# The weight decode by way of a PSUM bank, and another table of ranks, in an attention and two-FFN kernel

## The chip, the cores and the metric

One core of a Trainium2 chip. The metric is the device time of one launch in microseconds; a kernel's time is the median of its runs.

## The reference

Four batches of eight heads, sequence 1152, head width 64. Queries are averaged in pairs, so 576 rows of queries meet 1152 keys. The attention's output, 2304 tokens of width 512, goes through two feed-forward layers.

```python
q_pool = q.reshape(B, H, S // 2, 2, D).mean(axis=3)
scores = scale * np.matmul(q_pool, k.transpose(0, 1, 3, 2))
attn = np.exp(scores - max); attn = attn / (sum + 1e-09)
x = (attn @ v) as (B * S/2, H * D)
g = s * relu(x @ w_in) ** 2 + b;  x = g @ w_out            # d_ff 2048
out = (1 / (1 + exp(-(x @ w_gate))) * (x @ w_val)) @ w_out2  # d_ff 1536
```

## The kernel before

All matmuls run on operands that are split in two, a high part and the rest, and each product is made of three matmuls (high by high, high by low, low by high; `mm3`, lines 537 to 540). The five weight matrices arrive as 64-bit floats, in pairs of 32-bit words, and are decoded on the chip.

**The decode** (`decode`, line 481) handles one tile of 128 x 512 weights. A DMA on SP's queue brings the words into a buffer `raw` (three of them). Then, on the upper words, a clamp on GpSimd or VectorE ("w top", line 496) and a multiplication by a power of two on ScalarE ("w scale", line 499, in place); on the lower words a shift on VectorE ("w low", line 500); then two steps on VectorE that put the bits together: "w join" (line 503) and "w sign" (line 506). Both read the scaled upper words and the lower words and write the lower words. "w hi" (line 462) and "w lo" (line 472) split the result into the tile `w` that TensorE loads. There are 104 decodes: 32 for the first feed-forward layer in batch 0, whose results are also written to DRAM ("w keep") and fetched from there for the other batches ("w fetch", line 520, issued on GpSimd's queue), and 72 for the second layer.

**The order** of all instructions on all engines is written by a planner when the program is built. Each step is added with an engine, a duration, what it reads and writes, and a rank. `Plan.order` (line 229 on) walks through time; a free engine takes, among its ready steps for which buffers are free (`fits`, line 242), the one with the lowest rank. The base ranks are FE 0 (feed-forward), DE 0.5 (decode), AT 1 (attention), SK 2, FP 3. The table `MOVED` (line 42 on) has for each named step a pair that is added to the rank and to the place in the list. A step with the flag `port` on VectorE is held back while GpSimd is busy, and taken then only if no other step is ready (lines 272 to 286); a GpSimd step waits for the end of such a VectorE step (line 281).

**PSUM** has eight banks of 128 x 512 words. The planner hands them out by tag; a tag has a limit of its own (`ROOM`: ps 4, pr 8, pm 1, acc 5, ff 6, p2 3), and all together take at most eight. Tags in `LOOSE` may be taken out of turn.

**The course.** Batch 0's attention runs with rows of queries on the partitions (`pair_rows`, tags pr and acc), batches 1 to 3 with keys on the partitions (`scores`, `half_head_sums`, tags ps, pm, acc). The first layer (`ffn1`, tag ff) of batch b is put between the attention of batch b + 1. When the attention is done, `ffn2` (tag p2) handles batches 0 and 1, then `ffn1` handles batch 3, then `ffn2` batches 2 and 3. From about 840 us on there is no attention.

Of the kernel before, what the change touches and what calls it, by code (L numbers as in the profile page):

```python
# [11 lines left out]
F32 = mybir.dt.float32  # L12
F32R = mybir.dt.float32r
AF = mybir.ActivationFunctionType
ALU = mybir.AluOpType
U32 = mybir.dt.uint32
# [9 lines left out]
    w=4, raw=3, xy=2, xx=1, r=2, g=4,  # L26
    qn=1, kn=1, vn=1, qT=2, kT=2, vt=2, st=6, pp=6,
    sg=2, mx=2, mc=2, r9=1, x=1, s=2, rs=1, rr=1,
    yy=1, yl=1, h=4, fo=9,
    ps=4, pr=8, pm=1, acc=5, ff=6, p2=3, bank=8,  # L30
)

DIRECT = (1, 2)
BANKS = {"pr", "ps", "pm", "acc", "ff", "p2"}
LOOSE = {"pr", "ps", "ff", "p2", "r"}


MOVED = {
    "q load": (-0.5, 114),
    "k load": (46, 79),  # L40
    "v load": (58.5, 89),
    "v hi": (-18, -97),
    "v lo": (60, -156),
    "q add": (0, -97),
    "q twice": (0, -7),
    "pr qT": (0, 53),
    "pr q hi False": (23, -93),
    "pr q lo False": (24.5, 3),
    "pr q hi True": (45.5, 50),
    "pr q lo True": (5, 36),  # L50
    "pr kT": (-5, 44),
    "pr k hi": (2, -112),
    "pr k lo": (-5, 116),
    "s b load": (15, 94),
    "r qk 1": (0, 35),
    "r max": (36, 97),
    "r - max": (-29, -40),
    "r exp": (60, -57),
    "r pT": (-23, 13),
    "r p": (0, 52),  # L60
    "r p hi": (17, -107),
    "r p lo": (-25.5, -51),
    "r pv": (-38, 107),
    "r pT hi": (0, 70),
    "r pT lo": (47, -75),
    "r o": (-40, 39),
    "r x add": (40, -62),
    "r qk 2": (-1.5, -71),
    "r sums": (0.5, 106),
    "r sums eps": (-4, 9),  # L70
    "r 1 / sums": (-8, 75),
    "r spread": (-38, 44),
    "r rows": (0, -92),
    "r rows mid": (0, 108),
    "r x / sums": (-1.5, 74),
    "r x / sums mid": (60, 35),
    "r end": (0, 96),
    "ps qT": (24, 13),
    "ps q hi False": (60, 90),
    "ps q lo False": (6, -123),  # L80
    "ps kT": (10, 16),
    "ps k hi": (36.5, -29),
    "ps k lo": (-1, 88),
    "xx hi": (58, -86),
    "xx lo": (2.5, 93),
    "w load": (-12, 6),
    "w top": (-17, 81),
    "w scale": (-3, 17),
    "w low": (-20.5, -68),
    "w join": (9, 116),  # L90
    "w sign": (-25.5, -42),
    "w hi": (-40, 42),
    "w lo": (-28.5, -87),
    "w keep": (-1, 29),
    "one": (-39, -96),
    "ff xx up": (58, 135),
    "ff relu": (0, 72),
    "square": (-40, 76),
    "g hi": (27.5, -76),
    "g lo": (-10.5, 98),  # L100
    "ff down": (57, 43),
    "ff y": (9, 84),
    "column sum": (0, -65),
    "ff y add": (15.5, 115),
    "bias": (13.5, -34),
    "y bias": (-3, 137),
    "y store": (-33, -12),
    "qk": (44.5, 68),
    "s copy": (34.5, 24),
    "s max": (14, 33),  # L110
    "max T": (0, 53),
    "max": (20.5, 103),
    "max rows": (41.5, -120),
    "s - max": (14.5, 67),
    "exp": (0, -7),
    "p hi": (-40, -44),
    "p lo": (-7.5, -102),
    "pv hi": (-10.5, -118),
    "pv lo": (49.5, -31),
    "sums": (41, -60),  # L120
    "x": (36.5, 0),
    "sums out": (10, -13),
    "sums in": (5, -102),
    "1 / sums spread": (-16.5, 16),
    "1 / sums out": (60, -32),
    "1 / sums in": (2.5, -82),
    "x / sums": (0, 63),
    "1 / sums": (27.5, -20),
    "w fetch": (-35.5, -18),
    "w come": (-20.5, 6),  # L130
    "x store": (44, -24),
    "turn": (20, -21),
    "yy load": (-40, -79),
    "yy hi": (0, 50),
    "yy lo": (0, -39),
    "p2 yy up": (4.5, 6),
    "gate": (8, -90),
    "gate val": (-25.5, -72),
    "h hi": (0.5, 90),
    "h lo": (-40, -43),  # L140
    "down 2": (-21, 31),
    "out": (-5, -6),
    "out add": (0, -59),
    "out store": (-2, 45),
    "xx load": (0, 48),
    "p2 xx up": (0, -49),
    "p2 relu": (0, -7),
    "p2 down": (0, 24),
    "p2 y": (-10, -68),
    "p2 y add": (40, -54),  # L150
}


# [193 lines left out]
def kernel(  # L347
# [14 lines left out]
    nc = tc.nc  # L362
# [25 lines left out]

    plan = Plan(ROOM, LOOSE, BANKS, MOVED)

# [5 lines left out]
    ones, zero, eps = (values[:, i:i + 1] for i in range(3))  # L396
# [7 lines left out]
    bias = const.tile([P, KC], F32, name="bias")  # L404
# [14 lines left out]
    def slot(pool, tag, shape, dtype=F32, view=lambda t: t):  # L419
        uid[0] += 1  # L420
        name = f"{tag}_{uid[0]}"
        return plan.slot(tag, lambda k: view(pools[pool].tile(shape, dtype, tag=f"{tag}{k}", bufs=1, name=name)))
# [9 lines left out]
    def bank(tag):  # L432
        return plan.slot(tag, lambda k: banks[:, k])
# [13 lines left out]
    def act(name, n, issue, r, w, rank, sbuf=True):  # L447
        plan.add(name, "ACT", (95 if sbuf else 50) + 0.833 * n, issue, r, w, rank)

    def dve(name, n, issue, r, w, rank, fast=False, port=None):  # L450
        plan.add(name, "DVE", 70 + (0.52 if fast else 1.04) * n, issue, r, w, rank, port=fast if port is None else port)

    def shared(name, n, issue, r, w, rank, pool, act=None, fast=False, more=0):

        other = {"DVE": 70 + (0.52 if fast else 1.04) * n} if act is None else {"ACT": 95 + act * n}
        alts = {**{e: t + more for e, t in other.items()}, "POOL": 105 + pool * n + more}
        plan.add(name, alts, 0, issue, r, w, rank, port=True)

    def copy_sb(name, n, out, in_, r, w, rank):
        def issue(e):  # L460
            if e == "ACT":
                nc.scalar.copy(out=out(), in_=in_())  # L462
            else:
                nc.gpsimd.tensor_scalar(out=out(), in0=in_(), scalar1=1.0, scalar2=0.0, op0=ALU.mult, op1=ALU.add)

        shared(name, n, issue, r, w, rank, 0.95, act=0.833)
# [4 lines left out]
    def tt_sb(name, n, out, in0, in1, op, r, w, rank):  # L471
        shared(name, n, lambda e: ENGINE[e].tensor_tensor(out=out(), in0=in0(), in1=in1(), op=op), r, w, rank, 2.15)  # L472
# [4 lines left out]
    def dma(name, n_bytes, issue, r, w, rank):  # L477
        plan.add(name, "SP", max(n_bytes / 360.0, 500), issue, r, w, rank)


    def decode(src, w, gate, rank):

        raw = slot("dec", "raw", [P, 512, 2], U32)
        low, top = (raw, 0), (raw, 1)

        def words(i):
            return raw.t[:, :, i]

        def fetch():
            if len(src.shape) == 3:  # L490
                nc.sync.dma_start(out=raw.t.rearrange("p (k f) t -> p k (f t)", f=P), in_=src)
            else:
                nc.sync.dma_start(out=raw.t.rearrange("p f t -> p (f t)"), in_=src)

        dma("w load", P * 4096, fetch, gate, [low, top], rank)
        shared("w top", 512, lambda e: ENGINE[e].tensor_scalar(  # L496
            out=words(1).bitcast(F32), in0=words(1).bitcast(F32), scalar1=F64_TOP, scalar2=-F64_TOP, op0=ALU.min, op1=ALU.max,
        ), [], [top], rank, 1.08, fast=True)
        act("w scale", 512, lambda: nc.scalar.mul(words(1).bitcast(F32), words(1).bitcast(F32), 2.0 ** -112), [], [top], rank)  # L499
        dve("w low", 512, lambda: nc.vector.tensor_scalar(  # L500
            out=words(0), in0=words(0), scalar1=29, scalar2=None, op0=ALU.logical_shift_right,
        ), [], [low], rank, True)
        dve("w join", 512, lambda: nc.vector.scalar_tensor_tensor(
            out=words(0), in0=words(1), scalar=3, in1=words(0), op0=ALU.logical_shift_left, op1=ALU.bitwise_or,
        ), [top], [low], rank, port=True)
        dve("w sign", 512, lambda: nc.vector.scalar_tensor_tensor(
            out=words(0), in0=words(1), scalar=0x80000000, in1=words(0), op0=ALU.bitwise_and, op1=ALU.bitwise_or,
        ), [top], [low], rank, port=True)
        copy_sb("w hi", 512, lambda: w.t[:, 0, :], lambda: words(0).bitcast(F32), [low], [(w, 0)], rank)
        tt_sb("w lo", 512, lambda: w.t[:, 1, :], lambda: words(0).bitcast(F32), lambda: w.t[:, 0, :].bitcast(F32), ALU.subtract,  # L510
              [low, (w, 0)], [(w, 1)], rank)
# [69 lines left out]
    def load_x(b):  # L581
        return load_split("fx", "xx", x_d[b], [("x_d", b, i) for i in range(2 * NP)])
# [503 lines left out]
    for i, (b, hp) in enumerate(pairs):  # L1086
# [11 lines left out]
        if hp == NP - 1 and b < B - 1:  # L1098
            if b + 1 in DIRECT:
                xs[b + 1] = slot("fx", "xy", [P, KC, SQ])  # L1100
            y = ffn1(b, load_split("fx", "xx", None, None, here=xs[b]) if b in xs else load_x(b))
# [9 lines left out]
    y = ffn1(B - 1, load_x(B - 1))  # L1111
# [33 lines left out]
```

## Time and profile before

| | |
|---|---|
| median of three runs | 1452.34 us (1451.93 to 1453.6) |
| profiled execution, its own time | 1457.94 us |
| its span, first to last instruction | 1456.2 us |
| TensorE (PE) busy | 1381.1 us, 95% of the span |
| VectorE (DVE) busy | 1069.8 us, 73% |
| ScalarE (ACT) busy | 936.4 us, 64% |
| GpSimd (POOL) busy | 762.1 us, 52% |
| mean granted TensorE clock | 0.99 |

Shares over the whole span are means over stages. Until about 400 us all four engines are busy 70 to 90% of the time, then TensorE comes close to full, and from 840 us on the other engines have half of the time or more free. Matmuls are pipelined, so the duration of one is longer than the distance to the next. Idle time of an engine is put down to the last thing that it waited for.

### The profile page before, as it was taken

To read this page: it belongs to the slowest core of one execution; us is meant where nothing else is said; L and a number is where in the kernel's file an instruction comes from. 1 tells how busy PE (TensorE), PEld (TensorE's weight loads), DVE (VectorE), ACT (ScalarE), POOL (GpSimd) and SP (SyncE) were. 2 spreads that over 40 slices of the span, in tenths; PEclk is the share of its full clock that TensorE was granted. 3 is DMA by queue.
4 is the path that set the end of the run, shared out by engine and by line. 5 is a ranking of instruction groups with operands and counts; after the bars stand their busy time and mean duration, and the time that the engine had idled before them with its cause. 6 is when DMAs were issued, how large, how long until landed. Compare 5 with 4: busy or idle time off the path is not lost.

```text
span 1456.2 us, 24999 instructions
## 1 busy us (share of the span) xinstructions
PE 1381.1 (95%) x9164; PEld 1315.3 (90%) x9164; DVE 1069.8 (73%) x1780; ACT 936.4 (64%) x2004; POOL 762.1 (52%) x664
## 2 busy tenths in 40 slices
PE   7988999888999999999999989999999999999998
PEld 6877989887888999999899989999898999989897
DVE  6899899888998889889998856747475126738552
ACT  6899889778798999888888735434141534434130
POOL 3678577667776557565755434525353004526230
PEclk9999999999999999999999999999999999999999
DMA  3336134454433342233341363312236444313112
GB/s 90 93 121 200 31 101 124 155 157 149 154 109 136 87 140 75 84 103 121 95 140 42 121 260 131 101 59 87 73 100 230 163 172 145 117 48 126 34 69 65
DMA packets 103043, 167.88 MB, mean 115 GB/s; under 512 B 44652, under 2 KB 80264, under 8 KB 93832
## 3 DMA queue, kind: packets, MB, share of 16 engines
q1 hardware_dynamic: 96008, 115.95, 25.9%
q0 software_dynamic: 6912, 50.33, 9.8%
q8 instruction: 72, 1.18, 0.3%
q14 instruction: 51, 0.42, 0.1%
HBM read 139.99 MB, written 26.28 MB: 114 GB/s over the span
## 4 chain that ended last, share of the span: by engine, by line
PE 50%; ACT 8%; DVE 4%; issue 3%; DMA 2%; POOL 2%; SPq 0%; DVEq 0%; POOLq 0%; ACTq 0%
PE banks L538 11%; PE banks L540 11%; PE banks L539 11%; PE banks L1047 3%; PE banks L1048 3%; PE banks L1046 3%; PE banks L768 3%; ACT st L794 2%; PE banks L816 1%; ACT st L469 1%; PE banks L821 1%; PE banks L817 1%; DVE mx L475 1%; ACT pp L462 1%; DMA w<-d_1u_1u 1%
## 5 line engine op out<-in xcount | busy, mean ns | idle before, releaser
L472 POOL TENSOR_TENSOR pp<-st,pp 128x864 fp32r<-128x864 f32 x82 | 174.9, 2137 | 42.4 <-ACT pp L462 31.6
L540 PE MATMUL banks<-yy,w 128*128 128x384 f32 x576 | 192.6, 334 | 0.3 <-POOL w L472 0.3
L538 PE MATMUL banks<-yy,w 128*128 128x384 f32 x576 | 192.5, 334 | 0.0
L539 PE MATMUL banks<-yy,w 128*128 128x384 f32 x576 | 192.5, 334 | 0.0
L469 ACT COPY st<-banks 128x288 f32<-128x288 f32 x432 | 151.3, 409 | 39.9 <-PE banks L768 32.4
L768 PE MATMUL banks<-qT,kT 128*128 128x288 f32 x864 | 161.4, 304 | 3.2 <-DVE mx L475 2.7
L475 DVE TENSOR_TENSOR mx<-banks,mx 128x288 f32<-128x288 f32 x336 | 150.7, 449 | 18.1 <-ACT st L469 7.0
L538 PE MATMUL banks<-xx,w 128*128 128x288 f32 x512 | 155.1, 303 | 8.1 <-DMA w<-d_1u_1u 5.1
L539 PE MATMUL banks<-xx,w 128*128 128x288 f32 x512 | 152.4, 298 | 0.0
L540 PE MATMUL banks<-xx,w 128*128 128x288 f32 x512 | 152.4, 298 | 0.0
L475 DVE TENSOR_TENSOR st<-st,banks 128x864 f32<-128x864 f32 x144 | 148.9, 1043 | 2.4 <-PE banks L746 1.5
L538 PE MATMUL banks<-g,w 128*128 128x288 f32 x448 | 135.1, 302 | 3.3 <-DVE mx L475 2.1
L794 ACT ACTIVATE st<-st 128x864 f32<-128x864 f32 x144 | 132.0, 927 | 7.0 <-DVE st L475 6.4
L496 POOL TENSOR_SCALAR raw<-raw 128x512 f32<-128x512 f32 x99 | 77.4, 782 | 109.1 <-DMA raw<-in_moe_w_out_dram 40.6
L816 PE MATMUL banks<-pp,vt 128*128 128x288 f32 x432 | 123.6, 306 | 11.0 <-ACT pp L462 7.3
L768 PEld LDWEIGHTS banks<-qT,kT 128*128 128x128 f32 x864 | 127.9, 190 | 6.0 <-DVE mx L475 4.2
L539 PE MATMUL banks<-g,w 128*128 128x288 f32 x448 | 132.5, 296 | 0.0
L540 PE MATMUL banks<-g,w 128*128 128x288 f32 x448 | 132.5, 296 | 0.0
L817 PE MATMUL banks<-pp,vt 128*64 128x288 f32 x432 | 119.8, 297 | 0.0
L499 ACT ACTIVATE raw<-raw 128x512 f32<-128x512 f32 x104 | 71.1, 685 | 71.8 <-POOL raw L496 66.0
L540 PEld LDWEIGHTS banks<-yy,w 128*128 128x128 f32 x576 | 108.1, 188 | 0.6 <-POOL w L472 0.6
L538 PEld LDWEIGHTS banks<-yy,w 128*128 128x128 f32 x576 | 108.1, 188 | 0.3
(147 smaller groups left out, 3952.4 us busy)
## 6 DMA issues: line engine op xcount, KB each, us to landing
w<-d_1u_1u POOLq DMA_DIRECT2D x24, 1024.0 KB, 5.6
w<-d_1d_1d POOLq DMA_DIRECT2D x24, 1024.0 KB, 6.6
raw<-in_moe_w_out_dram SPq DMA_DIRECT2D x40, 512.0 KB, 3.9
raw<-in_moe_w_gate_dram SPq DMA_DIRECT2D x24, 512.0 KB, 12.7
raw<-in_moe_w_val_dram SPq DMA_DIRECT2D x24, 512.0 KB, 3.8
qn<-in_q_dram SPq DMA_DIRECT2D x16, 576.0 KB, 3.7
kn<-in_k_dram SPq DMA_DIRECT2D x32, 288.0 KB, 3.9
vn<-in_v_dram SPq DMA_DIRECT2D x32, 288.0 KB, 2.8
```

Source lines behind the costliest of these rows:

```text
L469: act(name, n, lambda: nc.scalar.copy(out=out(), in_=in_()), r, w, rank, sbuf=False)
L472: shared(name, n, lambda e: ENGINE[e].tensor_tensor(out=out(), in0=in0(), in1=in1(), op=op), r, w, rank, 2.15)
L475: dve(name, n, lambda: nc.vector.tensor_tensor(out=out(), in0=in0(), in1=in1(), op=op), r, w, rank)
L496: shared("w top", 512, lambda e: ENGINE[e].tensor_scalar(out=words(1).bitcast(F32), in0=words(1).bitcast(F32), scalar1=F64_TOP, scalar2=-F ...
L499: act("w scale", 512, lambda: nc.scalar.mul(words(1).bitcast(F32), words(1).bitcast(F32), 2.0 ** -112), [], [top], rank)
L538: nc.tensor.matmul(ps(), lhsT=whi(), rhs=xhi(), start=first, stop=False)
L539: nc.tensor.matmul((ps_lo or ps)(), lhsT=whi(), rhs=xlo(), start=False, stop=False)
L540: nc.tensor.matmul(ps(), lhsT=wlo(), rhs=xhi(), start=False, stop=last)
L768: nc.tensor.matmul(ps.t[:, :HQ], lhsT=kT.t[:, c], rhs=qq[:, w, hf * HQ:(hf + 1) * HQ], start=(w == 0), stop=(w == 1))
L794: act("exp", 3 * HQ, lambda s=s: nc.scalar.activation(out=s.t, in_=s.t, func=AF.Exp), [], parts, AT)
L816: nc.tensor.matmul(acc.t[:, :HQ], lhsT=vt.t[:, 3 * i + c, D:], rhs=hi.t[:, c], start=(i == c == 0), stop=False)
L817: nc.tensor.matmul(acc.t[:D, :HQ], lhsT=vt.t[:, 3 * i + c, :D], rhs=hi.t[:, c], start=False, stop=False)
```

## The change

"w scale" no longer writes in place: it writes a PSUM bank of a new tag `wd`, at most two at a time, within the eight. "w join" and "w sign" read that bank in place of the upper words in SBUF, and lose the flag `port`. So a decode holds a bank from its scale to its sign. The tag is added to `BANKS` and `LOOSE`. The table `MOVED` is another one; of its 108 or so pairs nearly all differ. The rows that the text speaks of stand below.

```diff
-    ps=4, pr=8, pm=1, acc=5, ff=6, p2=3, bank=8,
+    ps=4, pr=8, pm=1, acc=5, ff=6, p2=3, wd=2, bank=8,
-BANKS = {"pr", "ps", "pm", "acc", "ff", "p2"}
-LOOSE = {"pr", "ps", "ff", "p2", "r"}
+BANKS = {"wd", "pr", "ps", "pm", "acc", "ff", "p2"}
+LOOSE = {"wd", "pr", "ps", "ff", "p2", "r"}
...
-    "q load": (-0.5, 114),
-    "k load": (46, 79),
-    "v load": (58.5, 89),
+    "q load": (-11.5, -108),
+    "k load": (5, -106),
+    "v load": (43, -19),
...
-    "w load": (-12, 6),
-    "w top": (-17, 81),
-    "w scale": (-3, 17),
-    "w low": (-20.5, -68),
-    "w join": (9, 116),
-    "w sign": (-25.5, -42),
-    "w hi": (-40, 42),
-    "w lo": (-28.5, -87),
+    "w load": (-23, 31),
+    "w top": (-28, -10),
+    "w scale": (14, -116),
+    "w low": (-29.5, 69),
+    "w join": (-4.5, -70),
+    "w sign": (-32, 58),
+    "w hi": (-35, -102),
+    "w lo": (-30.5, 18),
...
-    "w fetch": (-35.5, -18),
-    "w come": (-20.5, 6),
+    "w fetch": (37, 122),
+    "w come": (-32, -69),
...
         low, top = (raw, 0), (raw, 1)
+        scaled = bank("wd")
...
-        act("w scale", 512, lambda: nc.scalar.mul(words(1).bitcast(F32), words(1).bitcast(F32), 2.0 ** -112), [], [top], rank)
+        act("w scale", 512, lambda: nc.scalar.mul(scaled.t, words(1).bitcast(F32), 2.0 ** -112), [top], [scaled], rank)
...
         dve("w join", 512, lambda: nc.vector.scalar_tensor_tensor(
-            out=words(0), in0=words(1), scalar=3, in1=words(0), op0=ALU.logical_shift_left, op1=ALU.bitwise_or,
-        ), [top], [low], rank, port=True)
+            out=words(0), in0=scaled.t.bitcast(U32), scalar=3, in1=words(0), op0=ALU.logical_shift_left, op1=ALU.bitwise_or,
+        ), [scaled], [low], rank)
         dve("w sign", 512, lambda: nc.vector.scalar_tensor_tensor(
-            out=words(0), in0=words(1), scalar=0x80000000, in1=words(0), op0=ALU.bitwise_and, op1=ALU.bitwise_or,
-        ), [top], [low], rank, port=True)
+            out=words(0), in0=scaled.t.bitcast(U32), scalar=0x80000000, in1=words(0), op0=ALU.bitwise_and, op1=ALU.bitwise_or,
+        ), [scaled], [low], rank)
```

## Rows read from the trace of the kernel before

**Rows 1.** The page, engines: busy us, share of the span, instructions.

```profile
PE 1381.1 (95%) x9164; PEld 1315.3 (90%) x9164; DVE 1069.8 (73%) x1780; ACT 936.4 (64%) x2004; POOL 762.1 (52%) x664
```

**Rows 2.** Stages: stretch, length; busy us (instructions) of each engine; granted clock, DMA share, GB/s.

```profile
0.00:40.00 40.00, 29.86 (x181) 26.92 (x181) 26.40 (x61) 26.82 (x79) 14.56 (x26) 0.96 0.31 82
40.00:400.00 360.00, 321.04 (x2280) 300.31 (x2280) 319.20 (x612) 307.11 (x739) 255.13 (x236) 0.98 0.42 129
400.00:840.00 440.00, 424.44 (x3157) 409.41 (x3156) 387.44 (x635) 382.15 (x790) 269.76 (x195) 1.00 0.33 105
840.00:1440.00 600.00, 594.49 (x3503) 569.32 (x3502) 332.88 (x466) 219.76 (x397) 222.61 (x209) 1.00 0.35 118
```

**Rows 3.** PE's waits, 40 to 400: engine line waited for: us, times, longest.

```profile
PE banks L816 <- ACT pp L462: 6.3, 6, 2.0
PE banks L899 <- ACT st L913: 4.5, 7, 1.2
PE banks L538 <- DVE mx L475: 4.3, 2, 2.2
...
PE banks L899 <- DVE g L475: 1.6, 3, 0.8
PE banks L702 <- ACT r L611: 1.6, 1, 1.6
PE banks L702 <- DVE kT L475: 1.6, 2, 1.4
...
PE banks L702 <- DVE g L475: 1.3, 2, 0.9
...
PE banks L1002 <- ACT st L913: 0.2, 1, 0.2
```

**Rows 4.** Groups, 40 to 400: count, busy us, mean ns of one, idle before.

```profile
L503 DVE SCALAR_TENSOR_TENSOR raw<-raw 128x512 uint32<-128x512 uint32 x32 | 27.3, 872 | 0.2
L506 DVE SCALAR_TENSOR_TENSOR raw<-raw 128x512 uint32<-128x512 uint32 x32 | 26.2, 833 | 0.0
L499 ACT ACTIVATE raw<-raw 128x512 f32<-128x512 f32 x32 | 22.1, 690 | 10.1 <-POOL raw L496 9.8
```

**Rows 5.** Groups, 840 to 1440, the same columns.

```profile
L503 DVE SCALAR_TENSOR_TENSOR raw<-raw 128x512 uint32<-128x512 uint32 x72 | 61.5, 863 | 9.4 <-ACT raw L499 9.1
L506 DVE SCALAR_TENSOR_TENSOR raw<-raw 128x512 uint32<-128x512 uint32 x72 | 63.0, 891 | 0.3
```

**Rows 6.** Line 506, whole span: duration ns min/median/max, first and last start us.

```profile
L506 DVE SCALAR_TENSOR_TENSOR raw<-raw x104: 674/685/1892, 78.6 to 1402.5; 128x512 uint32<-128x512 uint32 x104
```

**Rows 7.** Timeline of POOL and of DVE at 102 us: start, us, instruction.

```profile
102.23 1.44 POOL L472 TENSOR_TENSOR qn<-qn 128x576 f32<-128x576 f32 x1
102.69 1.52 DVE L506 SCALAR_TENSOR_TENSOR raw<-raw 128x512 uint32<-128x512 uint32 x1
```

**Rows 8.** DVE steps with one operand in PSUM: duration ns min/median/max.

```profile
L475 DVE TENSOR_TENSOR fo<-banks,fo x36: 677/692/692, 1024.7 to 1451.4; 128x512 f32<-128x512 f32 x36
L645 DVE SCALAR_TENSOR_TENSOR xy<-banks,s_sb,xy x96: 500/508/520, 283.5 to 1231.0; 128x288 f32<-128x288 f32 x96
```

**Rows 9.** Groups of ACT, 40 to 400: a copy of 512 columns out of PSUM.

```profile
L469 ACT COPY pp<-banks 128x512 f32<-128x512 f32 x14 | 8.0, 605 | 0.0
```

**Rows 10.** Timelines of ACT and DVE: first and last scale, first and last sign of 32.

```profile
73.47 0.73 ACT L499 ACTIVATE raw<-raw 128x512 f32<-128x512 f32 x1
...
78.62 0.68 DVE L506 SCALAR_TENSOR_TENSOR raw<-raw 128x512 uint32<-128x512 uint32 x1
...
384.91 0.71 ACT L499 ACTIVATE raw<-raw 128x512 f32<-128x512 f32 x1
...
398.75 0.67 DVE L506 SCALAR_TENSOR_TENSOR raw<-raw 128x512 uint32<-128x512 uint32 x1
```

**Rows 11.** PE's waits, 840 to 1160; and the page, DMA issues: KB, us to landing.

```profile
PE banks L538 <- DMA w<-d_1u_1u: 5.1, 2, 3.8
...
w<-d_1u_1u POOLq DMA_DIRECT2D x24, 1024.0 KB, 5.6
```

More of the change, by code (lines that the diff above doesn't have):

```diff
@@ L29 @@
     yy=1, yl=1, h=4, fo=9,
-    ps=4, pr=8, pm=1, acc=5, ff=6, p2=3, bank=8,
+    ps=4, pr=8, pm=1, acc=5, ff=6, p2=3, wd=2, bank=8,
 )
 DIRECT = (1, 2)
-BANKS = {"pr", "ps", "pm", "acc", "ff", "p2"}
-LOOSE = {"pr", "ps", "ff", "p2", "r"}
+BANKS = {"wd", "pr", "ps", "pm", "acc", "ff", "p2"}
+LOOSE = {"wd", "pr", "ps", "ff", "p2", "r"}
 MOVED = {
-    "q load": (-0.5, 114),
-    "k load": (46, 79),
-    "v load": (58.5, 89),
[L42 to L60, printed above, removed]
-    "r p hi": (17, -107),
[L62 to L85, printed above, removed]
-    "w load": (-12, 6),
-    "w top": (-17, 81),
-    "w scale": (-3, 17),
-    "w low": (-20.5, -68),
-    "w join": (9, 116),
-    "w sign": (-25.5, -42),
-    "w hi": (-40, 42),
-    "w lo": (-28.5, -87),
[L94 to L128, printed above, removed]
-    "w fetch": (-35.5, -18),
-    "w come": (-20.5, 6),
[L131 to L150, printed above, removed]
@@ new lines @@
+    "q load": (-11.5, -108),
+    "k load": (5, -106),
+    "v load": (43, -19),
+    "v hi": (0, -58),
+    "v lo": (-14.5, -90),
+    "q add": (-12, 88),
+    "q twice": (-11.5, -101),
+    "pr qT": (0, 49),
+    "pr q hi False": (-5, -7),
+    "pr q lo False": (0, -55),
+    "pr q hi True": (-18.5, -85),
+    "pr q lo True": (-2, -90),
+    "pr kT": (-13, 96),
+    "pr k hi": (-8.5, -139),
+    "pr k lo": (-27, -102),
+    "s b load": (57, 145),
+    "r qk 1": (0, -13),
+    "r max": (2.5, 28),
@@ new lines @@
+    "r - max": (0, 65),
+    "r exp": (40, -55),
+    "r pT": (-40, -82),
+    "r p": (-6, -99),
+    "r p hi": (17, -107),
+    "r p lo": (-29, 116),
+    "r pv": (-16, -20),
+    "r pT hi": (3.5, 77),
+    "r pT lo": (20, -109),
+    "r o": (-16, -19),
+    "r x add": (14.5, 7),
+    "r qk 2": (-17, -3),
+    "r sums": (40, 106),
+    "r sums eps": (0, 8),
+    "r 1 / sums": (0, -88),
+    "r spread": (-35, -35),
+    "r rows": (-14.5, 84),
+    "r rows mid": (0, 138),
+    "r x / sums": (28.5, 60),
@@ new lines @@
+    "r x / sums mid": (58, -101),
+    "r end": (0, -142),
+    "ps qT": (-7, -19),
+    "ps q hi False": (60, 9),
+    "ps q lo False": (-26.5, -18),
+    "ps kT": (-12, -99),
+    "ps k hi": (25.5, 19),
+    "ps k lo": (-27, -122),
+    "xx hi": (52.5, -114),
+    "xx lo": (60, 5),
+    "w load": (-23, 31),
[6 more added lines that the diff above has]
+    "w lo": (-30.5, 18),
+    "w keep": (-1, 44),
@@ new lines @@
+    "one": (-31, 12),
+    "ff xx up": (54, -89),
+    "ff relu": (-8, -16),
+    "square": (-40, 68),
+    "g hi": (15.5, 65),
+    "g lo": (-14, -120),
+    "ff down": (31.5, -82),
+    "ff y": (5, 32),
+    "column sum": (-12.5, -26),
+    "ff y add": (-12, 32),
+    "bias": (0, -22),
+    "y bias": (0, 6),
+    "y store": (-0.5, 76),
+    "qk": (0, -116),
+    "s copy": (27.5, -93),
+    "s max": (-5, 78),
+    "max T": (-40, 115),
+    "max": (0, -187),
+    "max rows": (-4.5, 109),
+    "s - max": (60, 136),
@@ new lines @@
+    "exp": (1.5, 87),
+    "p hi": (-35.5, 91),
+    "p lo": (-6, 74),
+    "pv hi": (-23, 14),
+    "pv lo": (0, -91),
+    "sums": (0, 103),
+    "x": (38.5, -32),
+    "sums out": (13, -64),
+    "sums in": (-18, 86),
+    "1 / sums spread": (-24.5, 54),
+    "1 / sums out": (55.5, 24),
+    "1 / sums in": (52.5, -30),
+    "x / sums": (8, -98),
+    "1 / sums": (48.5, -15),
+    "w fetch": (37, 122),
+    "w come": (-32, -69),
+    "x store": (-0.5, -60),
+    "turn": (-20, -75),
+    "yy load": (7, 89),
@@ L151 @@
+    "yy hi": (43, 60),
+    "yy lo": (9.5, 97),
+    "p2 yy up": (20, 46),
+    "gate": (0, 42),
+    "gate val": (-34.5, 17),
+    "h hi": (-23, 46),
+    "h lo": (-15.5, 113),
+    "down 2": (-39.5, -53),
+    "out": (0, -79),
+    "out add": (29.5, 68),
+    "out store": (0, -87),
+    "xx load": (0, -57),
+    "p2 xx up": (-4, -69),
+    "p2 relu": (0, -107),
+    "p2 down": (0, 32),
+    "p2 y": (-1, -117),
+    "p2 y add": (-0.5, -40),
 }
```

## The prediction

> **What bounds the kernel now.** I read the page first: TensorE is busy for 1381.1 of 1456.2 us, and no other engine comes near it [rows 1]. The stage table says where the missing 75 us are [rows 2]: 10 us of the first 40, 39 us of the stretch 40 to 400, 16 us of 400 to 840, 6 us of 840 to 1440, and the rest in the last 16 us. From 840 on nothing that another engine saves can be seen in the time: TensorE is busy 594.5 of 600 us there, VectorE 333. The stretch 40 to 400 is the open one: TensorE 321 of 360 us, VectorE 319, ScalarE 307, GpSimd 255. No engine is full; they wait for one another in short steps. The list of TensorE's waits in that stretch has 24 rows that sum to 38.1 us, and the 14 of them that name VectorE sum to 19.0 [rows 3]. So I price what the change does by stretch, and only 40 to 400 counts: 32 of the 104 decodes lie there, 72 lie in 840 to 1440 [rows 4, 5].
>
> **Part 1, join and sign read PSUM.** Before, both read two operands from SBUF. Half of the signs take 674 to 685 ns, but the longest took 1892 [rows 6]; one of the long ones is in the timeline beside a GpSimd step: the sign that starts at 102.69 takes 1.52 us and ends at 104.21, 0.54 us after GpSimd's step ends at 103.67, as if it had done most of its work only then [rows 7]. Their means in 40 to 400 are 872 and 833 ns [rows 4]. VectorE steps with one operand in PSUM show no such tail: 677 to 692 ns over 36 additions of 512 columns, 500 to 520 ns over 96 steps of the same operation of 288 columns [rows 8]. I take 690 ns for the new join and sign. That frees 32 x (872 - 690 + 833 - 690) = 10.4 us of VectorE in 40 to 400, and 72 x (863 - 690 + 891 - 690) = 26.9 us in 840 to 1440, where it is worth nothing [rows 2, 4, 5]. How much of the 10.4 us reaches the end? Between 0 (VectorE idles 41 us there already) and 10.4. Half of what TensorE waits for in the stretch is VectorE, 19.0 of 38.1 [rows 3], so I take half: **-5.2 us**. GpSimd is relieved in turn where it would have been the one that stands behind; its 255 of 360 us make it no bound, and I put that at 0.
>
> The rows let a PSUM operand cost 690 - 685 = 5 ns over an undisturbed SBUF step. [...]
>
> **Part 2, the scale writes PSUM.** It takes 690 ns from SBUF to SBUF [rows 4]. No step of ScalarE in the trace writes PSUM. The nearest rows: 605 ns when the same 512 columns are read from PSUM [rows 9]. So the new duration may be 85 ns lower, and as nothing excludes a loss, 85 ns higher: 32 x 85 ns = 2.7 us either way, at most half of it seen, +-1.4. I take 0, since 690 is the row of the same source and size. [...]
>
> **Part 3, a PSUM bank per decode.** New: the bank is taken when the scale starts and free when the sign ends, and the next matmul that gets that bank waits for the sign on VectorE. Before, 32 pairs of a scale and its sign lie in 40 to 400, from 73.47 to 79.30 for the first and from 384.91 to 399.42 for the last [rows 10]; their sum is 437 us, 13.7 each. Held as long, banks would lose 437 of 8 x 360 = 2880 bank-us, 15%. But the distance before is made by the order, not by need: a join whose `port` flag is set goes, in `Plan.order` (lines 272 to 286), only when GpSimd is free or nothing else is ready, and GpSimd is busy 71% of this stretch. The change takes that flag from join and sign; and its table moves the scale later (-3 to 14) and the join and the sign earlier (9 to -4.5, -25.5 to -32). The three steps then stand close: the sum of three is 0.69 + 0.69 + 0.69 = 2.1 us, and with a wait of one step of up to 1 us before each of the two, 4 us. So 32 x 2.1 to 4 = 67 to 128 bank-us, 2 to 4.5% of 2880. What is behind it: TensorE's waits for the reader of a bank (exp 4.5, the running maximum 4.3, the splits of g 1.6 + 1.3 and of kT 1.6, relu 1.6: about 15 us [rows 3]). 4.5% of these is 0.7 us; 4.5% of TensorE's 321 us, the other end, is 14 us. I take **+1**, near the lower end, because TensorE's waits and not its whole work hang on free banks. In 840 to 1440 the tag p2 takes three of eight banks, two more stand free for the decode: 0.
>
> **Part 4, the other table of ranks.** It touches nearly every step, so it changes the order on all engines and on SP's and GpSimd's queues, where the loads of q, k, v and w move forward and the fetch of kept weights moves back (-35.5 to 37). The trace of before can't show that order. Bounds: it can win or lose at most what the order costs now and again: half of the 38.1 us of waits in 40 to 400, so -19 to +19. I take **-4**, a tenth: joins that no longer stand behind GpSimd give back the raw buffers sooner, so later loads and decodes have more room, and the loads' ranks move forward with them. This is the weakest term.
>
> **Sum.** -5.2 + 0 + 1 - 4 = -8.2 us. The profiled execution took 1457.94 us (span 1456.2), 5.6 us above the median 1452.34; it would come to 1449.7, and the median to **1444**. With half of part 1 either way and part 2's ends its own range is 1438 to 1449.
>
> **The rivals.**
> - *The order gains more.* The table wins the whole 19 us: -5.2 + 1 - 19 = -23, 1429. For it: 54 us of TensorE's idle time lie between 40 and 840 [rows 2]. Against: many small causes, none over 6.3 us [rows 3].
> - *Hidden anyway.* VectorE's 10.4 us become idle time, since steps of the softmax chain wait for ScalarE and TensorE in turn (6.3 us of TensorE's waits are for ScalarE's split [rows 3]), and the order is worth nothing: 1450 to 1455.
> - *Slower by banks.* If the decode holds its bank as long as scale and sign lie apart now, the loss is 15% of 321 us, 48 us, times the share of bank waits in the waits, 15 of 38.1: 19 us. Less 5.2 that is +14, 1466. It decides where 19 x hold / 13.7 passes 5.2, at a hold of 3.7 us without any gain from the table, and at 6.6 us with its 4. For it: `pr` and `acc` fill all eight banks while b = 0. Against: the flag that made the distance is gone, and the three ranks have moved together.
> - *Slower by late weights.* The fetch of kept weights drops by 72 ranks on GpSimd. A fetch lands in 5.6 us, and TensorE waited for it twice, 5.1 us [rows 11]. If half of the 12 chunks of the three later passes show as much as one of those, 2.55 us, that is +15, and with the -8.2 about +7: 1459.
>
> **How the numbers follow.** Forecast 0.47; order gains more 0.15; hidden 0.14; banks 0.14; late weights 0.10. A measurement of this kernel can tell 0.2%, some 3 us, from no change. Faster: 0.47 + 0.15 = 0.62; same 0.14; slower 0.24. Range 1431 to 1461: the best of the larger gain and the worst of the banks are left out, about 0.17.
>
> **What would show it.** Right: join and sign at 0.68 to 0.70 us with no tail; VectorE's busy time lower by some 35 us; scale to sign under 5 us in the early stretch; TensorE's idle time in 40 to 400 down from 39 to about 31 us; the span from 840 on unchanged. Wrong: matmuls in the early stretch that wait for the sign or for a scale's bank, waits of L538 for w from DRAM, or an early stretch as long as before with VectorE emptier.

## The result

The changed kernel took 1469.9 us (median of four runs, 1463.4 to 1473.2) beside 1453.0 us: 1.0108 times the time before, with a 95% interval of 1.007 to 1.0146. Run once more against 18 runs of the kernel before, it gave 1469.6 against 1454.3 us, 1.0100 (1.0073 to 1.0128). Some 16 us slower, where 8 us faster was forecast; the time lies above the range's upper end of 1461.

What the profile after shows comes from two executions: the first (1463.4 us, the fastest of its kernel) and that of the second run (1469.2 us, close to the median). The page of the first, engines, answers to [rows 1]:

```profile
span 1461.6 us, 25022 instructions
PE 1381.0 (94%) x9164; PEld 1311.1 (90%) x9164; DVE 1040.9 (71%) x1797; ACT 926.8 (63%) x1986; POOL 737.2 (50%) x665
```

TensorE has the same work. VectorE is busy 28.9 us less (1069.8 before, and some 35 less were forecast), and yet the span grew. Where, is seen with stages cut a little differently from [rows 2]. First the kernel before, five stretches (length; busy us and instructions of PE, PE's loads, DVE, ACT, POOL; granted clock, DMA share, GB/s):

```profile
40.00:450.00 410.00, 368.96 (x2631) 345.61 (x2631) 365.28 (x697) 353.27 (x830) 291.67 (x260) 0.98 0.41 128
450.00:660.00 210.00, 201.38 (x1500) 194.35 (x1498) 183.84 (x311) 187.11 (x396) 125.94 (x92) 0.99 0.33 101
660.00:720.00 60.00, 57.57 (x431) 55.14 (x430) 54.52 (x89) 54.05 (x110) 43.79 (x32) 1.00 0.37 115
720.00:1100.00 380.00, 373.46 (x2372) 361.40 (x2371) 266.50 (x375) 194.18 (x375) 181.10 (x155) 1.00 0.33 109
1100.00:1180.00 80.00, 78.58 (x516) 73.95 (x515) 22.89 (x32) 28.70 (x54) 13.91 (x18) 1.00 0.61 211
```

Then the changed kernel, its second profile:

```profile
40.00:450.00 410.00, 374.45 (x2655) 347.50 (x2654) 360.60 (x702) 356.43 (x834) 297.74 (x272) 0.98 0.41 128
450.00:660.00 210.00, 199.49 (x1471) 191.52 (x1470) 177.90 (x304) 177.53 (x371) 115.24 (x86) 0.99 0.32 101
660.00:720.00 60.00, 52.23 (x374) 50.41 (x373) 48.74 (x73) 47.63 (x98) 39.25 (x28) 0.94 0.33 106
720.00:1100.00 380.00, 374.83 (x2401) 361.96 (x2400) 254.16 (x392) 198.96 (x386) 174.31 (x155) 1.00 0.33 111
1100.00:1180.00 80.00, 73.41 (x457) 68.97 (x456) 23.96 (x35) 25.90 (x48) 15.74 (x19) 0.96 0.58 196
```

Read the count of PE's matmuls, a rough measure of progress, since they differ in size. In 40 to 450 the change is ahead by 24 matmuls, in 450 to 660 behind by 29: about even by 660. Then two short stretches lose most: 374 matmuls for 431 in 660 to 720, and 457 for 516 in 1100 to 1180, where TensorE idles 7.8 and 6.6 us (2.4 and 1.4 before) and its granted clock falls to 0.94 and 0.96. Between the two, 29 matmuls are won back. The 57 and 59 that are missed there are worth some 7.5 us each, an estimate at 132 ns (304 matmuls fill the 40 us from 1160 to 1200, where TensorE is full). The first profile loses in the same two stretches, 379 and 466 matmuls, and is ahead by 65 in 40 to 450. PE's waits of the changed kernel in 600 to 1180 (us in total, times, longest), second profile:

```profile
PE banks L539 <- DMA w<-d_1u_1u: 9.5, 2, 6.6
PE banks L817 <- POOL pp L464: 6.6, 2, 6.1
```

The first answers to [rows 11], where it was 5.1 us, longest 3.8.

**The gap near 675 us** (near 668 in the first profile). ScalarE stands 5.03 us before it may copy a result into `x` (start, us, instruction; idle before it):

```profile
673.69 1.21 ACT L723 ACTIVATE qT<-banks 128x256 fp32r<-128x256 f32 x4
679.93 0.39 ACT L469 COPY x<-banks 64x288 f32<-64x288 f32 x1 [5.03 <-DMA x_d<-x]
680.35 0.92 ACT L795 ACTIVATE st<-st 128x864 f32<-128x864 f32 x1
```

`x` is one buffer, and its last content was still being stored. That store had been issued at 671.22, right after GpSimd had issued two fetches of weights of 1 MB each (SP's and POOL's timelines):

```profile
671.22 0.33 SPq L874 DMA_DIRECT2D x_d<-x  x1
...
669.89 1.15 POOL L521 DMA_DIRECT2D w<-d_1d_1d  x2
```

So 8.7 us passed from the issue of this store of 144 KB to the copy that waited for it. On ScalarE the exp followed the copy, at 680.35; the split on GpSimd that waited for the exp began at 681.44, 6.78 us idle before it; and TensorE's L817 waited 6.1 us for that split. The packets in the trace, told apart by queue and size, show what the store shared the DMA engines with: the 256 packets of the two fetches run from 671.20 to 678.92, and the 128 packets of the store among them, from 674.92 to 679.01, 4.1 us. In the kernel before no fetch is under way beside the same store, and its 128 packets take 0.9 us (672.42 to 673.29). In the changed kernel's first profile the store's packets take 4.3 us (667.05 to 671.34), among those of the fetches (663.28 to 671.25). No run took the fetches away.

**The gap near 1140 us** (near 1134 in the first profile). In the changed kernel SP's queue has eight output stores, each of which waits for its result, ahead of the load of `yl`; in the kernel before the load went first:

```profile
1105.92 0.50 SPq L659 DMA_DIRECT2D y_d<-xy  x1
1108.97 14.91 SPq L1062 DMA_DIRECT2D out_dram<-fo  x8
1123.92 0.59 SPq L550 DMA_DIRECT2D yl<-y_d  x1
```

```profile
1099.95 0.50 SPq L658 DMA_DIRECT2D y_d<-xy  x1
1106.85 0.34 SPq L549 DMA_DIRECT2D yl<-y_d  x1
```

The first of the two fences is the changed kernel, the second the kernel before: the load comes 18.0 us after the store of y against 6.9. The output stores are the smaller part of that. In e7 below the load stands right behind the store of y, and still comes 13.7 us after it, since it reads what the store writes:

```profile
1106.49 0.50 SPq L659 DMA_DIRECT2D y_d<-xy  x1
1120.22 0.34 SPq L550 DMA_DIRECT2D yl<-y_d  x1
```

The rest is the store itself. In the changed kernel two fetches of 1 MB are issued 0.5 us ahead of it, and its 128 packets of 9 KB run for 8.7 us (1110.60 to 1119.32), among those of the fetches (1107.89 to 1118.26) and of words for the decode; in the kernel before the two fetches are issued 1.6 us behind it, and its packets take 3.4 us (1102.78 to 1106.14). In the changed kernel's first profile they take 9.3 us (1103.88 to 1113.22), among those of the fetches (1101.31 to 1112.38). So in both gaps a store runs beside two fetches that the new order puts just ahead of it. GpSimd waits for `yl`, and the fetches of weights stand behind that in its queue (changed kernel):

```profile
1130.45 1.32 POOL L464 TENSOR_SCALAR yy<-yl 128x576 fp32r<-128x576 f32 x2 [12.55 <-DMA yl<-y_d]
1131.73 3.86 POOL L472 TENSOR_TENSOR yy<-yl,yy 128x576 fp32r<-128x576 f32 x2
1135.54 1.15 POOL L521 DMA_DIRECT2D w<-d_1d_1d  x2
1136.67 0.55 POOL L521 DMA_DIRECT2D w<-d_1u_1u  x1
```

**What the change does by itself** to the three steps came out as foreseen. Groups of the decode's steps, changed kernel, first profile, 40 to 450 (count, busy us, mean ns), to be set against [rows 4]:

```profile
L504 DVE SCALAR_TENSOR_TENSOR raw<-banks,raw 128x512 uint32<-128x512 uint32 x32 | 21.8, 684 | 0.5 <-ACT banks L500 0.2
L507 DVE SCALAR_TENSOR_TENSOR raw<-banks,raw 128x512 uint32<-128x512 uint32 x32 | 21.6, 682 | 0.1
L500 ACT ACTIVATE banks<-raw 128x512 f32<-128x512 f32 x32 | 20.8, 652 | 2.3 <-POOL raw L497 0.9 <-DVE qm L726 0.6 <-POOL g L464 0.4
```

Join 872 to 684 ns, sign 833 to 682, no tail (over all 104 the longest are 703 and 695 ns), scale 690 to 652. From the start of the scale to the end of the sign 4.7 us on the mean of the 32 early decodes (151 us in all) where it was 13.7. TensorE waits in 40 to 400 for the sign that holds its bank twice, 2.1 us:

```profile
PE banks L900 <- DVE raw L507: 1.5, 1, 1.5
...
PE banks L539 <- DVE raw L507: 0.6, 1, 0.6
```

### The profile page after: what moved, and what is told of

Same layout as the page of the kernel before. It is cut to its first block, busy times and chain, and to the rows that moved or that the text cites. A ratio compares the mean times of both kernels' runs of the same rounds, so it can differ in the third digit from the quotient of the medians.

```text
span 1461.6 us, 25022 instructions
## 1 busy us (share of the span) xinstructions
PE 1381.0 (94%) x9164; PEld 1311.1 (90%) x9164; DVE 1040.9 (71%) x1797; ACT 926.8 (63%) x1986; POOL 737.2 (50%) x665
## 4 chain that ended last, share of the span: by engine, by line
PE 59%; ACT 14%; DVE 12%; issue 6%; DMA 5%; POOL 2%; SPq 0%; DVEq 0%; ACTq 0%; POOLq 0%
PE banks L539 12%; PE banks L541 12%; PE banks L540 12%; PE banks L769 3%; DVE mx L475 3%; ACT st L795 3%; PE banks L1049 3%; PE banks L1048 3%; PE banks L1047 3%; ACT st L469 2%; PE banks L817 2%; ACT pp L462 2%; PE banks L818 2%; DVE kT L475 2%; PE banks L967 2%
## 5 line engine op out<-in xcount | busy, mean ns | idle before, releaser
L472 POOL TENSOR_TENSOR pp<-st,pp 128x864 fp32r<-128x864 f32 x87 | 183.3, 2109 | 53.8 <-ACT pp L462 44.3
L497 POOL TENSOR_SCALAR raw<-raw 128x512 f32<-128x512 f32 x103 | 82.2, 799 | 117.6 <-DMA raw<-in_moe_w_val_dram 45.6
L817 PE MATMUL banks<-pp,vt 128*128 128x288 f32 x432 | 123.3, 306 | 9.8 <-POOL pp L464 6.8
L500 ACT ACTIVATE banks<-raw 128x512 f32<-128x512 f32 x104 | 66.6, 642 | 83.1 <-POOL raw L497 79.4
L539 PEld LDWEIGHTS banks<-xx,w 128*128 128x128 f32 x512 | 97.5, 190 | 13.7 <-issue 7.6
L540 PEld LDWEIGHTS banks<-yy,w 128*128 128x128 f32 x576 | 108.1, 188 | 0.4
```

The source lines that it names most:

```text
L497: shared("w top", 512, lambda e: ENGINE[e].tensor_scalar(out=words(1).bitcast(F32), in0=words(1).bitcast(F32), scalar1=F64_TOP, scalar2=-F ...
L500: act("w scale", 512, lambda: nc.scalar.mul(scaled.t, words(1).bitcast(F32), 2.0 ** -112), [top], [scaled], rank)
L539: nc.tensor.matmul(ps(), lhsT=whi(), rhs=xhi(), start=first, stop=False)
L540: nc.tensor.matmul((ps_lo or ps)(), lhsT=whi(), rhs=xlo(), start=False, stop=False)
L817: nc.tensor.matmul(acc.t[:, :HQ], lhsT=vt.t[:, 3 * i + c, D:], rhs=hi.t[:, c], start=(i == c == 0), stop=False)
```

## The experiments

Two theories stood at the start. T: the PSUM path gains, and the order that the new table writes loses more, by transfers that land late. R: the banks that decodes hold, or the path itself, cost the time. The edits below are to the changed kernel or to the kernel before, as said. Where the planner's input is touched it writes a new order; where it says "same order", each engine's list is the same but for what is named.

### The two halves crossed

```diff
 # e1: the changed kernel
-MOVED = { ... the table of after }
+MOVED = { ... the table of before }
 # e2: the kernel before
-MOVED = { ... the table of before }
+MOVED = { ... the table of after }
```

> The changed kernel with the table of ranks of before: scale into a PSUM bank, join and sign from it. The planner writes an order anew, so its luck is part of it. Theory T (the new table's order, by two transfers that land late at about 668 and 1134 us, costs the time; the PSUM path gains): about the time of before or less, 1443 to 1456. Rival R (the banks that the decodes hold cost the time): 1462 or more, with matmuls in 40 to 400 us that wait for the sign.

> The kernel before with the new table of ranks: the decode stays in SBUF. Theory T: slow by the order, 1460 to 1480, with waits of TensorE for late transfers in the trace, though the planner writes another order than in the changed kernel since the held-back steps differ. Rival R: no banks are held, so not above 1458.

Measured: 1486.2 us (1.0228, 1.0205 to 1.025) and 1485.4 us (1.0215, 1.0198 to 1.0232). The halves alone lose 33 and 32 us, and both together 16. By its number e1 speaks for R; e2 lies above T's range, and far above R's. Neither theory foresaw both. The sign that R named is weak in e1: matmuls wait 2.7 us for the sign in 40 to 400, against 2.1 in the changed kernel. The decode's steps in e1 are as short as in the changed kernel (join 682, sign 681 ns, scale to sign 4.1 us), so its loss is not in them. In e2 they are not short, though the flag `port` is set (40 to 450):

```profile
L503 DVE SCALAR_TENSOR_TENSOR raw<-raw 128x512 uint32<-128x512 uint32 x32 | 36.7, 1157 | 0.1
L506 DVE SCALAR_TENSOR_TENSOR raw<-raw 128x512 uint32<-128x512 uint32 x32 | 35.1, 1103 | 0.0
```

Against the 872 and 833 ns of [rows 4] that is 32 x (1157 - 872 + 1103 - 833) = 17.8 us of VectorE: a part of what the new table costs the old code is a longer stall of the very steps that part 1 priced. What the pair shows is that code and table can't be priced apart: with the old table the code costs 33 us, and the new table then gives 17 back. That each table was fitted to its code is a guess so far; e9 to e11 below test it.

### The path alone, at one order

e3 keeps the changed kernel's order, and the planner's banks, and only sends the words the old way:

```diff
-... nc.scalar.mul(scaled.t, words(1).bitcast(F32), 2.0 ** -112) ...
+... nc.scalar.mul(words(1).bitcast(F32), words(1).bitcast(F32), 2.0 ** -112) ...
 # join and sign, both
-... in0=scaled.t.bitcast(U32), ...
+... in0=words(1), ...
```

> The changed kernel's own order, instruction for instruction on every engine and with the same banks kept free, but the scale writes in place and join and sign read SBUF, as before. What differs is only the path. Theory T: join and sign get their tail back (means 850 to 900 ns for 690), time 0 to 10 us above the changed kernel's 1470, and the two gaps of TensorE near 668 and 1134 us stay. Rival R in the form that the PSUM accesses themselves disturb TensorE: below 1463.

Measured: 1507.9 us, 1.037 (1.0355 to 1.0386). At this order the PSUM path is worth 1507.9 - 1469.6 = 38 us, far more than the 0 to 10 expected. R in the form that the PSUM accesses disturb TensorE, which had e3 below 1463, falls. The steps, 40 to 450:

```profile
L504 DVE SCALAR_TENSOR_TENSOR raw<-raw 128x512 uint32<-128x512 uint32 x32 | 40.8, 1279 | 0.3
L507 DVE SCALAR_TENSOR_TENSOR raw<-raw 128x512 uint32<-128x512 uint32 x32 | 36.5, 1144 | 0.1
```

They take 1279 and 1144 ns, much longer than the 872 and 833 of [rows 4]. Of these 64 steps 44 take more than 0.75 us, and every one of the 44 runs beside a step of GpSimd; in the kernel before it is 18 of 64, again all beside GpSimd, and of the 64 there 37 run beside a step of GpSimd, while the 27 others take at most 0.694 us. In the changed kernel's first profile 60 of the 64 run beside a step of GpSimd, and none takes more than 0.71 us. So the old order kept the two steps off GpSimd more than this one does. That is 32 x (1279 - 684 + 1144 - 682) = 33.8 us of VectorE. The first store of y, where batch 0's first layer is done, gives how much of it reached the course of the kernel; e3, then the changed kernel's second profile, then the kernel before (SP's timeline, all three):

```profile
476.17 0.33 SPq L659 DMA_DIRECT2D y_d<-xy  x1
...
445.39 0.33 SPq L659 DMA_DIRECT2D y_d<-xy  x1
...
447.00 0.33 SPq L658 DMA_DIRECT2D y_d<-xy  x1
```

476.17 - 445.39 = 30.8 us are seen there, against 33.8 of VectorE. It is not one for one: the granted clock of 40 to 450 is lower in e3, 0.96 for 0.98, which is up to 8 us of the 30.8 (an estimate, 410 x 0.02).

```profile
40.00:450.00 410.00, 353.79 (x2433) 324.69 (x2432) 367.33 (x645) 331.65 (x779) 285.81 (x254) 0.96 0.38 121
```

By the same store the changed kernel stands 1.6 us ahead of the kernel before, and it gains 24 matmuls on it in 40 to 450: most of what the path gives in the early stretch is used up by the order. (Between two orders that store is not the same place in the work; in e11 below, which is as fast as the changed kernel, it comes at 461.8.)

### The two gaps mended, at one order

```diff
 # x: the buffer of batch 3 has two tiles by turns (half 0, half 1)
-x = slot("sm", "x", [P, HQ]) if ...
+x = plan.slot("x", lambda k: pools["sm"].tile([P, HQ], F32, tag=f"x{hf}", bufs=1, ...)) if ...
 # yl: in the finished order, the load of yl for batch 2 is moved ahead
+to = (place of the last "y store" ahead of it) + 1
+out.insert(to, out.pop(at))
```

e4 has both edits, e6 the first alone, e7 the second alone; e5 is the changed kernel once more.

> The changed kernel's own order with two edits: the buffer x of batch 3 has two tiles by turns, so that the copy into it need not wait for the store of the one before; and the load of yl for batch 2 stands in SP's queue right behind the store of y, ahead of the output stores. Theory T: both gaps go, 6.2 + 6.9 us of idle TensorE and some 2.5 us at the lower clock: 1470 - 15.6 = 1454, between 1449 and 1458. Rival R: within 3 us of the changed kernel, 1466 to 1473.

> The changed kernel once more, for its spread: its four times lay between 1463.4 and 1473.2 and the profiled execution was the fastest of them. Theory T1 (the executions differ by when transfers land): median 1466 to 1473, and a profile whose early stretch, 40 to 400 us, is slower than in the first profile by some of the 9 us that the mended version lost there with the same order. Rival: the first profile is typical, TensorE's work at 600 us stands within 2 us of it, and the difference between the profile and the median comes from the two gaps alone.

> The changed kernel's order with the second tile for x alone. Theory T: the gap near 668 us goes, the one near 1134 stays: 3 to 8 us below the changed kernel, 1462 to 1467. Rival: the whole gain of the mended version was the other edit: 1468 to 1472.

> The changed kernel's order with the load of yl ahead of the output stores alone. Theory T: the gap near 1134 us shrinks to under 3 us, the one near 668 stays: 3 to 8 us below the changed kernel, 1462 to 1467. Rival: 1468 to 1472.

Measured: e5 1469.6 us; e6 1465.6 us (1.0071, 1.0052 to 1.009); e7 1465.8 (1.0064, 1.0043 to 1.0085); e4 1460.9 (1.0052, 1.0038 to 1.0067). By the medians the edits give 4.0, 3.8 and together 8.6 us. e4 ran beside other executions of the kernel before than e5 did; by the ratios (1.0100 for e5) it is 4.2, 5.2 and together 7.0 us. e4's interval lies below that of e5 (1.0073 to 1.0128), those of e6 and e7 overlap it. So the two gaps together are 7 to 9 of the 16 us, within the noise the sum of the two, and less than the 15.6 that I had counted from idle time and clock. e6 and e7 lie where T had them; e4's time lies 3 us above T's range. e4's stretches 660 to 720 and 1100 to 1180 hold 418 and 501 matmuls, against 374 and 457 in the changed kernel and 431 and 516 before, at a granted clock of 1.00 in both:

```profile
40.00:450.00 410.00, 372.98 (x2632) 345.57 (x2631) 358.86 (x699) 354.08 (x830) 295.37 (x269) 0.98 0.40 126
450.00:660.00 210.00, 199.11 (x1481) 191.34 (x1480) 179.59 (x304) 178.55 (x373) 117.47 (x88) 1.00 0.33 105
660.00:720.00 60.00, 56.25 (x418) 53.81 (x417) 54.34 (x83) 49.95 (x105) 41.28 (x29) 1.00 0.32 106
...
1100.00:1180.00 80.00, 77.28 (x501) 72.85 (x500) 24.92 (x37) 27.13 (x51) 15.72 (x19) 1.00 0.61 204
```

What is left against the kernel before are 19 matmuls in 450 to 660, and still 13 and 15 in the two mended stretches; 40 to 450 is level.

e5 settled a smaller question: the first profile was not typical. With the same lists, its first store of y came at 439.79, in e5 at 445.39. T1 put that down to when transfers land, which no row shows. What the traces do show is the clock: the decodes of the two drift apart in four steps of 1.0 to 1.8 us, around 105, 220, 295 and 335 us, and near each of them the granted clock of e5 falls, to 0.91 over 20 us, where the first profile keeps 1.00. Two of the four places, e5 and then the first profile:

```profile
100.00:120.00 20.00, 15.89 (x91) 12.96 (x91) 18.75 (x38) 16.55 (x45) 15.63 (x17) 0.91 0.54 181
280.00:300.00 20.00, 15.84 (x105) 14.62 (x104) 15.27 (x20) 16.16 (x31) 16.83 (x13) 0.91 0.59 193
...
100.00:120.00 20.00, 15.07 (x95) 12.30 (x94) 19.81 (x42) 16.97 (x45) 16.91 (x19) 1.00 0.62 207
280.00:300.00 20.00, 16.41 (x121) 15.20 (x121) 16.93 (x27) 17.74 (x34) 17.11 (x12) 1.00 0.74 241
```

Whether the clock makes the delay or follows from a wait just before it, the two traces don't settle.

### The old order, with the path where a bank was free

A decode can go through PSUM in the order of before where a bank is used by no other step from its scale to its sign. None of the 32 early decodes has such a bank; all 72 late ones do. e8 sends those 72 through PSUM, every engine's list unchanged:

```diff
-nc.scalar.mul(words(1).bitcast(F32), ...
+nc.scalar.mul(banks[:, LENT[raw]] if raw in LENT else words(1).bitcast(F32), ...
-in0=words(1), scalar=
+in0=banks[:, LENT[raw]].bitcast(U32) if raw in LENT else words(1), scalar=
```

> The kernel before with its own order on every engine, and the PSUM path for those decodes for which a bank is free from the scale to the sign in that order: all 72 of the second layer, none of the first 32. The prediction put those 72 at nothing, since TensorE is full there: 1450 to 1455, with 25 to 29 us less of VectorE. If VectorE's time counts there too, 1440 or less.

Measured: 1451.9 us against 1454.3, 0.998 (0.9962 to 0.9998), with VectorE's busy time in 840 to 1440 down from 332.88 to 302.20 us. Thirty microseconds of VectorE beside a full TensorE are worth 2.4 us, by the interval 0.3 to 5.5; the prediction had put them at nothing. It is the one version that is ahead of both kernels, by a little.

### How sharp a table is

```diff
 # e9, the kernel before          # e10, the kernel before      # e11, the changed kernel
-"s max": (14, 33)                -"exp": (0, -7)               -"w join": (-4.5, -70)
+"s max": (14.5, 33)              +"exp": (0.5, -7)             +"w join": (-4, -70)
 # e12, the changed kernel: the flag stays on join and sign
-[scaled], [low], rank)
+[scaled], [low], rank, port=True)
```

> The kernel before with one entry of its table moved by half a rank: s max from 14 to 14.5. The planner then writes another order from about line 650 of TensorE's list on. Theory F (the table is fitted to its code, so any new order is drawn from the many unfitted ones): 1462 to 1490. Rival G (most orders by this planner are alike, and the two crossed kernels were slow for what they cross): 1450 to 1459.

> The kernel before with exp moved from 0 to 0.5 in its table, a second draw; its order differs only later, from about 1790 of TensorE's list on. Theory F: 1458 to 1485. Rival G: 1450 to 1458.

> The changed kernel with w join moved from -4.5 to -4 in its table. Theory F: a new draw, 1472 to 1495, above the changed kernel's 1470. Rival G: 1460 to 1473.

> The changed kernel with the flag port left on join and sign, so that the planner keeps them off GpSimd as before although they read PSUM. If the flag sets how long a decode holds its bank (prediction, part 3): scale to sign in the early stretch 10 us or more in place of 4.7, and more waits of TensorE for the sign than 1.5 us; time 1480 or more. If the ranks set it: about 5 us and the time of any new order, 1470 to 1490.

Measured: e9 1475.8 us (1.0136, 1.0104 to 1.0168), e10 1464.6 (1.006, 1.004 to 1.0079), e11 1467.2 (1.0078, 1.0052 to 1.0104), e12 1499.1 (1.0303, 1.0259 to 1.0346). Half a rank on one of some hundred steps costs the kernel before 21 and 10 us, as F says. The changed kernel lost nothing by such a step: e11 lies at its own time, where F had 1472 or more. Three draws are few, but they agree with an old table that is a narrow best for its code, and a new one that is an order like its neighbour. For e9 the trace shows where a part of the 21 us comes from (40 to 450):

```profile
L503 DVE SCALAR_TENSOR_TENSOR raw<-raw 128x512 uint32<-128x512 uint32 x32 | 35.4, 1109 | 0.2
L506 DVE SCALAR_TENSOR_TENSOR raw<-raw 128x512 uint32<-128x512 uint32 x32 | 30.9, 971 | 0.0
```

With the flag set and half a rank on another step, join and sign are longer again: 32 x (1109 - 872 + 971 - 833) = 12.0 us more of VectorE. That they ran beside GpSimd, as every one over 0.75 us did in the kernel before and in e3, is likely here but was not counted. In e10 they take 877 and 840 ns, so its 10 us are something else. With the words in PSUM, e11 shows no such lengthening: they take 685 and 682. In e12 the distance from scale to sign is 9.7 us on the mean, 310 us in all, twice that of the changed kernel with the same ranks; in e1, with the old ranks and no flag, it is 4.1. With the flag it is 13.7 in the kernel before, 12.7 in e2 and 14.0 in e9. So the flag sets most of the distance, and the ranks little, as part 3 had it first. TensorE's waits for the sign grow only from 2.1 to 3.1 us. So the 29 us that e12 is slower than the changed kernel are not these waits; how far they come from the banks being away in the planner's count, and how far from another unfitted order, no run separates.

## Why the prediction was wrong

- **Part 4 is the step that failed: another order was priced at -4, with bounds of +-19, and added to part 1.** The bounds came from the reasoning that an order can win or lose at most half of what TensorE's waits cost now, 38.1 us. Orders lost more than that: the new table in the old code 32 us (e2), half a rank 21 (e9). And a new order does not come with the table alone: the tag `wd` and the dropped flag make the planner write another one too, and no term priced that. Parts 1 and 3 put the code at -4.2; with the old table it measured +33 (e1), and the new table then gave 17 us back, the sign that part 4 had. At one order, e3 parts the two: with the words kept in SBUF the changed kernel's order, which was written for the other path, costs 1507.9 - 1453.5 = 54 us, of which the path gives 38 back. The terms were added as if they were independent, while the value of the path hangs on the order.
- **Part 1, its size.** Right: no tail, 684 and 682 ns. The step that halved the gain, "half of what TensorE waits for in the stretch is VectorE", looks too low where it could be tested: of 33.8 us that VectorE loses in e3, 30.8 are seen at the first store of y, though the clock has a share in these. And the 10.4 us were the price of the path in the old order; in the new one it is three times that. A stall that an order avoids is small in its trace for that reason (18 of the 64 early steps over 0.75 us before, 44 in e3), and the trace of before could not say what the same steps cost elsewhere. What ran beside the long ones, the traces show: in 40 to 450 of the kernel before, join and sign with two operands in SBUF take up to 2.19 us beside a step of GpSimd and at most 0.694 us beside none; with one operand in PSUM they take at most 0.703 us beside one (first profile). The join's means are 1279 ns in e3 and 684 in the changed kernel.
- **PSUM against SBUF as a source.** 684 and 682 ns stand against 685 for the undisturbed SBUF step [rows 6], or 682, the median of the 27 early steps of the kernel before that ran beside no step of GpSimd. A PSUM operand cost these steps nothing that can be seen; 5 ns were allowed for it.
- **Part 2.** I took 0 of +-85 ns; it gained 38 ns (690 to 652) in the early stretch, and e3, with the same order and the words in SBUF, has 690 again. The gain is 32 x 38 ns = 1.2 us of ScalarE, too little to matter.
- **Part 3.** +1 us forecast, 2.1 us of direct waits for the sign measured. The distance from scale to sign, 4.7 us, is a little over the 2.1 to 4 that I worked out. I named both the flag and the ranks for it; e1 and e12 show that it is the flag.
- **The signs that it named.** TensorE's idle time in 40 to 400 went from 39 to 34.4 us in both profiles (busy 325.6 of 360), where 31 was forecast. That is near the -4.2 of parts 1 and 3, but by luck: it is what is left of a path that is worth some 31 us there at this order, and of an order that takes most of that back. The span from 840 on, which should have stayed unchanged, has the second gap. The sum's own range was also mis-added: half of part 1 and the ends of part 2 are 4.0 us either way, 1440 to 1448 and not 1438 to 1449.
- **The rival of late weights** had the right family and the wrong member. It foresaw waits of TensorE for fetched weights, and these grew from 5.1 to 9.5 us. But what delayed the fetch was not its own rank in the chunks of every pass: it was the load of `yl`, behind output stores on SP and behind a store of y that itself ran beside two other fetches; and the first gap was a store, not a load. Its price, 15 us, was near what happened for reasons that its text doesn't hold.
- **The rival of the banks** is not what the direct waits show: 2.1 us, not 19. What the lent banks cost by the order that the planner then writes stays open.

What is accounted for: of the 16 us, the two gaps 7 to 9 (e4). The rest, about as much, has no single cause that a run shows; in e4 it lies in 450 to 660 and in what is left of the two gaps. Why the early stretch gains only 24 matmuls, an estimated 3 us (65 and 9 us in the first profile), from a path worth some 31 us there at this order, and why the table gives no better order, isn't settled.

## What to carry to other kernels

A term that can't be read from the trace, "another order", must not be given a small value because it is unknown; where a planner writes the order from a fitted table, draw a few neighbours of the table first and take their spread as its price. Price a stall in the order in which it will run, not in one that was fitted to avoid it: the same join took 872 ns in one order, 1109 after half a rank on another step, and 1279 in the changed kernel's order. And when the order changes, look at the transfers first, for each one whose landing frees a single buffer, each load that reads what a store writes or stands behind stores on its queue, and what large transfers are issued just ahead of them.

## What the runs showed of the hardware

The clock's share of a gap: TensorE was idle for 7.8 and 6.6 us of the two stretches, and the granted clock of the two stretches was 0.94 and 0.96 in place of 1.00 (second profile). In the first profile, with the same two means, TensorE waits 6.19 us until 674.62 and 6.90 us until 1141.37, and the clock stands at 0.50 from 671.9 to 678.7 and from 1139.5 to 1146.4: within each gap it fell, and it stayed low for some 4 to 5 us of the work behind it, where matmuls of 288 columns start 0.24 us apart in place of 0.13. With the gaps mended (e4) both stretches have 1.00.

A small store beside large transfers: one store of 144 KB took 2.8 us from issue to landing in one place (the one landing of line 874 that the first profile gives); in another, where two fetches of 1 MB had been issued 1.3 us ahead, 8.7 us passed to the copy that waited for it (8.8 in the first profile). Its 128 packets took 4.1 us among those of the fetches, and 0.9 us in the kernel before.

Executions of one program differ: the same lists reached the first store of y at 439.8 and at 445.4 us, and the granted clock went with it, 1.00 and 0.98 over 40 to 450. The changed kernel's first four executions ran from 1463.4 us at a mean granted clock of 0.993 to 1473.2 us at 0.986. Which of the two comes first is not shown.

VectorE beside GpSimd: of 64 join and sign steps with both operands in SBUF 44 took longer than 0.75 us in e3, each beside a step of GpSimd, and the longest join of the whole run took 2.57; with one operand in PSUM 60 of the same 64 ran beside GpSimd and none took more than 0.71 us.
